# DFT over b and its inverse as eight array tiles of 64x32 and 32x64, with the spectral columns by parity of k

## The chip, the cores and the metric

The kernel runs on one core of a Trainium2 chip. The metric is the device time of one execution in microseconds (us). Engines are named as in the profile: PE is TensorE (PEld its weight loads), DVE is VectorE, ACT is ScalarE, POOL is GpSimd, SP is SyncE, which here only issues DMAs.

## The reference

Two branches work on the same x of 1 x 2048 x 512 in bf16, and a gate per row mixes them:

```python
g = sigmoid((x * gate_w).sum(-1, keepdims=True))
a = irfft2(rfft2(x, axes=(-2, -1)) * (w_r + 1j * w_i), s=(2048, 512)).astype(bfloat16)
h = einsum("bsd,df->bsf", x, w1) + b1            # d = 512, f = 1792
b = einsum("bsf,fd->bsd", h * tanh(softplus(h)), w2)
return g * a + (1 - g) * b
```

w_r and w_i are 2048 x 257, so branch a is a spectral filter over both axes; branch b is a dense layer with the Mish activation.

## The kernel before, in words

**Branch b** is dense. `mm1` (L810) multiplies w1 with the transposed x in four chunks of 512 rows, 14 row tiles each, four matmuls of 512 columns to a tile; ACT applies Mish (L819); `mm2` (L851, and L833 for the last row tile) multiplies back with 14 matmuls to each of 16 row tiles, in two parts of seven. Before the input is there, dummy matmuls (L509) keep PE going.

**Branch a** is the two-dimensional DFT as matmuls. The row index is s = 32a + b with 64 values of a and 32 of b.
- `tr` (L522) transposes x; DVE forms sums and differences (L537); `a1` (L551, L552, L554) is the real DFT over the 512 columns, 16 row tiles through PSUM bank 0, and eviction `e1` writes it to `In1` (in `Abuf`). The spectrum has 257 columns k; the real columns 0 and 256 are packed together, so that 256 are stored.
- `s1` (L572) is the DFT over a with its twiddle, in four batches, and gives 64 values e for every b. `e2` writes them to `Y1` (in `Ybuf`), and the DMAs `r1w` take them to DRAM (`scr1`) in four steps. `r1r` reads them back in another order into `In2` (in `Abuf`), so that b lies on the partitions.
- `s2` (L689) is the DFT over b in four batches n = 0 to 3, into PSUM banks 0 to 3. DVE multiplies by w_r and w_i (`wm`, L699, eight of 512 elements a batch), POOL or DVE adds or subtracts (`wz`, L705), and `s2i` (L732) is the inverse DFT over b, into the same banks. Eviction `e4` writes it to `T2s` (in `Ybuf`), the DMA `r2w` to DRAM (`scr2`), and eight DMAs `r2r` read it back as `T2r`.
- `s1i` (L764) and `a1i` (L776) are the inverses over a and over the columns; ACT scales by the gate (L781), DVE and POOL add the halves (L784), and branch b is added (L861, L869).

Columns k = 0 and 256 are real in the column direction and share a place; `s2x` (L664 to L666) separates them once, with small matmuls on the first column of `In2` and on its mirror image, which takes a reversed copy of the DFT matrix in `RR` (made by POOL in `rr`). DVE takes the result (`rs`, L711, and `x0`, L671 to L674), POOL multiplies it by the weights (`zq` to `z0i`), and `wc` (L722) writes it as column 0 of `Zb`, which `s2i` reads.

Before, the partitions of `In2` hold b (32) times real and imaginary part times two values of an index m2, and a matrix `RF` of 128 x 64 maps them to 32 outputs times the same two. Input and output with different m2 don't mix, so half of the matrix is zeros. `s2` uses it as two column halves of the array, `RI` of the inverse as two row halves:

```python
e.matmul(ps[64 * h:64 * h + 64, SB[i], 256 * c:256 * c + 256], RF[:, c, :], In2[:, 16 * h + u0 + i, :], ...)
```

with i over 4, c over 2 (real and imaginary output) and h over 2: sixteen matmuls of 256 columns a batch, in `s2` and in `s2i`.

**The order of the work** on each engine is fixed when the kernel is built. Each step is a task with an estimated time and with the buffers that it reads and writes; a list scheduler (`_Graph.schedule`) plays the engines and DMA queues through, takes among the steps that can start soonest the one of highest priority (the spectral steps stand above `mm1` and `mm2`), and so writes down each engine's order, which the engine then follows with semaphore waits. `evict` and `wz` may go to either of two engines, whichever is done first by the estimate. SP issues most of the DMAs in the order so planned: the input, `r1w`, `r1r`, two small ones of the gate (`gdj`), the constants of the inverse (`ld_g1`), `r2w`, `r2r` and the output. POOL issues the loads of the spectral weights (`ld_W`, into `WT`) and of w2.

Of the kernel before, what the change touches and what calls it, by code (L numbers as in the profile page):

```python
# [7 lines left out]
BF = mybir.dt.bfloat16  # L8
# [9 lines left out]
KR = 256  # L18

# [16 lines left out]
def _build_consts():  # L36
    cs = {}
# [21 lines left out]
    for kc in range(2):  # L59
        for half in range(2):  # L60
            kk = 4 * np.arange(64, dtype=np.float64)[:, None] + kc + 2 * half
            an = 2 * np.pi * kk * n / D
            GD[64 * half:64 * half + 64, 2 * kc, :] = 2 * np.cos(an)
            GD[64 * half:64 * half + 64, 2 * kc + 1, :] = -2 * np.sin(an)
# [5 lines left out]
    e = np.arange(64, dtype=np.float64)[None, :]  # L70
    M1 = np.zeros((128, 16, 2, 128))
    G1 = np.zeros((128, 32, 128))
    for b in range(32):
        bx, t = divmod(b, 16)
        ph = -2 * np.pi * e * (32 * a + b) / S
        c_, s_ = np.cos(ph), np.sin(ph)
        rows = slice(64 * bx, 64 * bx + 64)
        M1[rows, t, 0, 0:64] = c_
        M1[rows, t, 0, 64:128] = s_
        M1[rows, t, 1, 0:64] = -s_  # L80
        M1[rows, t, 1, 64:128] = c_
        ci, si = np.cos(-ph).T, np.sin(-ph).T
        G1[0:64, b, 0:64] = ci
        G1[64:128, b, 0:64] = -si
        G1[0:64, b, 64:128] = si
        G1[64:128, b, 64:128] = ci
    cs["M1"] = M1
    cs["G1"] = G1
    RF = np.zeros((128, 2, 64))
    RI = np.zeros((128, 2, 128))  # L90
    for b in range(32):
        for dd in range(32):
            ph = 2 * np.pi * b * dd / 32
            c_, s_ = np.cos(ph), np.sin(ph)
            for m2 in range(2):
                re_in, im_in = 4 * b + m2, 4 * b + 2 + m2
                o = 2 * dd + m2
                RF[re_in, 0, o] = c_
                RF[im_in, 0, o] = s_
                RF[re_in, 1, o] = -s_  # L100
                RF[im_in, 1, o] = c_
                for h in range(2):
                    i = 64 * h + o
                    RI[i, 0, re_in] = c_
                    RI[i, 0, im_in] = s_
                    RI[i, 1, re_in] = -s_
                    RI[i, 1, im_in] = c_
    P1 = np.zeros((128, 128))
    P0 = np.zeros((128, 128))

    def px(h, dd, m2):
        return 64 * h + 2 * dd + m2

    for h in range(2):
        for dd in range(32):
            for m2 in range(2):
                o = px(h, dd, m2)
                P1[px(1 - h, 31 - dd, 1 - m2), o] = 1
                u = 2 * m2 + h
                if u == 0:  # L120
                    P0[px(0, (32 - dd) % 32, 0), o] = 1
                else:
                    P0[px((4 - u) % 2, 31 - dd, (4 - u) // 2), o] = 1
    cs["SM"] = np.concatenate([RF.reshape(128, 128), RI.reshape(128, 256), P1, P0], axis=1)
# [198 lines left out]
def _build(nc, A_x, A_w_r, A_w_i, B_x, B_w1, B_b1, B_w2, gate_w, out):  # L323
# [6 lines left out]
    scr1 = nc.dram_tensor("scr1", (32, 128, KR), BF)  # L330
# [4 lines left out]
    with es:  # L335
# [13 lines left out]
        sm = sb("sm", [128, 640], BF)  # L349
# [18 lines left out]
        RR = sb("RR", [128, 2, 2, 64], BF)  # L368
# [12 lines left out]
        Zb = miscb[:, 4096:8192].rearrange("p (b u c n) -> p b u c n", b=2, u=4, c=2)  # L381
# [5 lines left out]
        RF = sm[:, 0:128].rearrange("p (c m) -> p c m", c=2)  # L387
        RI = sm[:, 128:384].rearrange("p (c m) -> p c m", c=2)
        P1m = sm[:, 384:512]
        P0m = sm[:, 512:640]  # L390
        In1 = Abuf[:, 0:8192].rearrange("p (t k) -> p t k", t=NT)
        In2 = Abuf[:].rearrange("p (j k) -> p j k", j=32)
        T2r = Abuf[:, 0:8192].rearrange("p (b k) -> p b k", b=32)
        Y1 = Ybuf[:].rearrange("p (b k) -> p b k", b=32)
        T2s = Ybuf[:, 0:8192].rearrange("p (h g k) -> p h g k", h=2, g=16)
# [8 lines left out]
        Wv = [w.rearrange("(m h g) k -> h m (g k)", h=2, g=16) for w in (A_w_r, A_w_i)]  # L404
        scr1_w = scr1.rearrange("b q k -> q b k")
        scr1_r = scr1.rearrange("b (m j) k -> (b m) j k", m=4)
        scr2_w = scr2.rearrange("b (m h g) k -> (b m) h (g k)", m=4, h=2)
# [85 lines left out]
        dma("ld_sm", sm[:], d_SM[:], writes=["sm"], nbytes=128 * 1280)  # L493
        dma("ld_gw", gwb[:, :], gate_w.unsqueeze(0).to_broadcast([128, 512]), writes=["gw"], nbytes=128 * 1024)
        dma("ld_gd", GDs[:], d_GD[:], writes=["GD"], nbytes=128 * 2048)
        for i in range(2):
            for h in range(2):
                dma(f"ld_W{i}{h}", WT[64 * h:64 * h + 64, i, :, :].rearrange("p g k -> p (g k)"), Wv[i][h],
                           writes=[("W", i, h)], nbytes=64 * 8224, queue="pool", deps=[t_w1])
        WALL = [("W", i, h) for i in range(2) for h in range(2)]  # L500
# [47 lines left out]
        for t in range(NT):  # L548
            def f_a1(e, t=t):
                pr = ps[:, 0, :].rearrange("p (r x) -> p r x", r=4)  # L550
                e.matmul(pr[:, 0, :], Tb[:, 0, t, :], FDs[:, 0:128], start=True, stop=True)  # L551
                e.matmul(pr[:, 2, :], Tb[:, 1, t, :], FDs[:, 128:256], start=True, stop=True)  # L552
                for i in range(2):
                    ins = e.matmul(pr[:, 1::2, :], Tb[:, 2 + i, t, :], FDs[:, 256 + 256 * i:512 + 256 * i].rearrange("p (r x) -> p r x", r=2),  # L554
# [5 lines left out]
            evict(f"e1_{t}", 512, In1[:, t, :].rearrange("p (c r q) -> p c r q", c=2, r=4),  # L560
                  ps[:, 0, :].rearrange("p (r c q) -> p c r q", r=4, c=2),
# [21 lines left out]
            if t % 4 == 3:  # L583
                for bx in range(2):
                    b0 = 16 * bx + t - 3
                    t_r1w.append(dma(f"r1w{t}_{bx}", scr1_w[:, b0:b0 + 4, :], Y1[:, b0:b0 + 4, :],
                                     reads=[("Y1", b0 + i) for i in range(4)], writes=[("scr1", b0 + i) for i in range(4)],
                                     nbytes=128 * 4 * 512, prio=SP0 + 1.0))
# [28 lines left out]
        def f_rr(e):  # L617
            v = RF.rearrange("p c (d m) -> p c d m", m=2)
            o = RR[:, 1].rearrange("p c (d m) -> p c d m", m=2)
            e.tensor_copy(out=RR[:, 0], in_=RF[:, :, ::-1])  # L620
            e.tensor_copy(out=o[:, :, :, 1], in_=v[:, :, ::-1, 1])
            e.tensor_copy(out=o[:, :, 0:1, 0], in_=v[:, :, 0:1, 0])
            return e.tensor_copy(out=o[:, :, 1:32, 0], in_=v[:, :, 31:0:-1, 0])

        G.add("rr", "pool", 1.2, f_rr, reads=["sm"], writes=["rr"])
# [16 lines left out]
        for hf in range(2):  # L642
            for h in range(2):
                j0 = 16 * h + 8 * hf
                t_r1r.append(dma(f"r1r{hf}{h}", In2[:, j0:j0 + 8, :], scr1_r[:, j0:j0 + 8, :],
                                 reads=[("scr1", b) for b in range(32)], writes=[("In2", j0 + i) for i in range(8)],
# [7 lines left out]
        SB = (0, 1, 2, 3)  # L654
        BSB = [("bank", i) for i in SB]
        xps = ps[:, 0, 0:64].rearrange("p (v c g) -> p v c g", v=2, c=2)

        def f_s2x(e):
            ins = None
            for c in range(2):  # L660
                for h in range(2):
                    o = xps[64 * h:64 * h + 64, :, c, :]
                    hr = 16 * (1 - h)
                    e.matmul(o[:, 0, :], RF[:, c, :], In2[:, 16 * h:16 * h + 16, 0], start=True, stop=True)  # L664
                    e.matmul(o[:, 1, 1:16], RR[:, 0, c, :], In2[:, hr + 15:hr:-1, 0], start=True, stop=True)
# [315 lines left out]
```

## Time and profile before

| what | value |
|---|---|
| three runs, median | 142.38 us (142.16 to 142.72) |
| the profiled execution | 142.56 us |
| its span, from the first to the last instruction | 140.8 us |
| PE busy | 136.2 us |
| DVE busy | 86.3 us |
| ACT busy | 81.4 us |
| POOL busy | 31.9 us |
| s2 (L689): 64 matmuls of 256 columns | 4.3 us busy |
| s2i (L732): 64 matmuls of 256 columns | 4.2 us busy |
| moved by DMA | 21.38 MB |

The profile is of one execution. A group of the profile is a line, an engine, an operation and its tiles; `128*64 128x256` is a matmul with a weight tile of 128 rows and 64 columns and a moving operand of 128 partitions by 256 columns. Matmuls overlap, and their ends are modelled, so their rate is read from the chain, from the starts, and not from the time of one. The chain that ended last is followed back from the last instruction, at each step to what released it; its times add up to the span.

### The profile page before, as it was taken

How to read it: one execution, taken by the hardware profiler on the slowest of the kernel's cores; microseconds unless marked ns; L12 is line 12 of the kernel's file. 1: busy time of each engine (PE TensorE's matmuls, PEld its weight loads, DVE VectorE, ACT ScalarE, POOL GpSimd, SP SyncE). 2: the span in 40 equal slices, each digit the busy share in tenths (PEclk: the TensorE clock that was granted, in tenths of full speed). 3: DMA queues.
4: the chain of work that ended last, by engine and by line, in shares of the span. 5: the costliest groups of instructions: out<-in, count | busy, mean ns of one | idle time of the engine just before them, and what ended most of it. 6: DMA issues, size and time to landing. Idle time of an engine off the chain costs nothing.

```text
span 140.8 us, 2515 instructions
## 1 busy us (share of the span) xinstructions
PE 136.2 (97%) x946; PEld 74.2 (53%) x946; DVE 86.3 (61%) x192; ACT 81.4 (58%) x128; POOL 31.9 (23%) x62
## 2 busy tenths in 40 slices
PE   6999999999999999999999999999999999999991
PEld 4756656455544435435445444544444666766670
DVE  0276757748999303983983893592200499999831
ACT  4448797969874487488058437532411685776300
POOL 4000670003000001560440440340000144256400
PEclk9999999999999999999999999999999999999999
DMA  3999999999705485700300300300359615333422
GB/s 87 334 382 387 393 245 214 239 333 366 222 8 154 151 254 202 289 0 10 143 0 0 149 0 5 149 2 0 143 150 277 179 27 119 80 79 92 98 52 58
DMA packets 16556, 21.38 MB, mean 152 GB/s; under 512 B 1248, under 2 KB 12384, under 8 KB 16160
## 3 DMA queue, kind: packets, MB, share of 16 engines
q1 hardware_dynamic: 15552, 17.22, 39.3%
q0 software_dynamic: 832, 3.94, 10.4%
q8 instruction: 7, 0.11, 0.3%
q10 hardware_dynamic: 160, 0.07, 0.2%
q14 instruction: 5, 0.04, 0.1%
HBM read 14.92 MB, written 6.29 MB: 151 GB/s over the span
## 4 chain that ended last, share of the span: by engine, by line
PE 92%; ACT 4%; DVE 0%; issue 0%
PE ps L810 33%; PE ps L851 32%; PE ps L776 5%; PE ps L509 3%; PE ps L689 3%; PE ps L572 3%; PE ps L732 3%; PE ps L764 3%; PE ps L522 2%; ACT Ybuf L452 2%; PE ps L833 2%; PE ps L554 2%; ACT act L819 1%; PE ps L551 1%; ACT Abuf L452 1%; ACT xT L452 1%
## 5 line engine op out<-in xcount | busy, mean ns | idle before, releaser
L810 PE MATMUL ps<-xT,w_sb 128*128 128x512 bf16 x224 | 54.2, 380 | 0.4 <-ACT act L819 0.3
L819 ACT ACTIVATE act<-ps,b1f 128x512 bf16<-128x512 f32 x56 | 38.1, 690 | 21.8 <-PE ps L810 16.4
L851 PE MATMUL ps<-w_sb,act 128*128 128x512 bf16 x210 | 48.3, 379 | 0.0
L810 PEld LDWEIGHTS ps<-xT,w_sb 128*128 128x128 bf16 x224 | 20.0, 98 | 24.1 <-ACT act L819 5.7
L851 PEld LDWEIGHTS ps<-w_sb,act 128*128 128x128 bf16 x210 | 20.1, 98 | 22.4 <-issue 0.4
L699 DVE TENSOR_TENSOR misc<-ps,WT 128x512 f32<-128x512 f32 x32 | 19.9, 685 | 12.6 <-PE ps L689 12.6
L705 POOL TENSOR_TENSOR misc<-misc 128x255 bf16<-128x255 f32 x16 | 11.4, 731 | 41.0 <-DVE misc L699 41.0
L784 POOL TENSOR_TENSOR Tg<-misc 128x256 bf16<-128x256 f32 x12 | 10.3, 873 | 27.9 <-ACT misc L781 27.9
L790 ACT ACTIVATE xo<-ps,omg 128x512 bf16<-128x512 f32 x11 | 7.6, 687 | 15.2 <-PE ps L851 15.0
L451 DVE CAST Ybuf<-ps 128x512 bf16<-128x512 f32 (+1 forms) x10 | 8.8, 900 | 9.3 <-PE ps L732 8.2
L781 ACT ACTIVATE misc<-ps,gcol 128x512 f32<-128x512 f32 x16 | 10.3, 685 | 5.0 <-PE ps L776 4.0
L451 DVE CAST misc<-ps 128x512 bf16<-128x512 f32 x8 | 5.5, 683 | 11.4 <-PE ps L764 11.4
L784 DVE TENSOR_TENSOR Tg<-misc 128x256 bf16<-128x256 f32 x20 | 12.0, 629 | 0.7 <-ACT misc L781 0.7
L594 DVE SCALAR_TENSOR_TENSOR junk<-xo,gwb 128x512 bf16<-128x512 bf16 x16 | 11.0, 689 | 0.7
L452 ACT ACTIVATE Ybuf<-ps 128x512 bf16<-128x512 f32 (+1 forms) x14 | 9.4, 718 | 2.6 <-PE ps L572 1.6
L451 DVE COPY xT<-ps 128x512 bf16<-128x512 bf16 x10 | 4.2, 424 | 9.1 <-PE ps L522 9.0
L776 PE MATMUL ps<-GDs,misc 128*128 128x256 bf16 x64 | 9.3, 273 | 0.0
L452 ACT ACTIVATE Abuf<-ps 128x512 bf16<-128x512 f32 x12 | 7.2, 602 | 0.0
L776 PEld LDWEIGHTS ps<-GDs,misc 128*128 128x128 bf16 x64 | 6.0, 98 | 2.3
L522 PEld LDWEIGHTS ps<-pid,xo 128*128 128x128 bf16 x64 | 5.2, 110 | 3.0 <-issue 0.4
L522 PE MATMUL ps<-pid,xo 128*128 128x128 bf16 x64 | 6.7, 242 | 0.0
L705 DVE TENSOR_TENSOR misc<-misc 128x255 bf16<-128x255 f32 x16 | 6.4, 441 | 0.0
(81 smaller groups left out, 115.7 us busy)
## 6 DMA issues: line engine op xcount, KB each, us to landing
scr<-Ybuf SPq DMA_DIRECT2D x8, 256.0 KB, 9.3
Abuf<-scr SPq DMA_DIRECT2D x4, 512.0 KB, 4.5
scr<-Ybuf SPq DMA_DIRECT2D x4, 512.0 KB, 3.0
Abuf<-scr SPq DMA_DIRECT2D x8, 256.0 KB, 5.3
w_sb<-in_B_w_dram POOLq DMA_DIRECT2D x2, 896.0 KB, 17.5
out_dram<-xo SPq DMA_DIRECT2D x14, 128.0 KB, 2.3
w_sb<-in_B_w_dram SPq DMA_DIRECT2D x3, 512.0 KB, 7.9
xo<-in_A_x_dram SPq DMA_DIRECT2D x3, 512.0 KB, 8.7
```

The lines of the kernel that those rows point to most:

```text
L451: G.add_multi(name, [("dve", dve_dur(n), lambda e: e.tensor_copy(out=dst, in_=src)), ("act", act_dur(n), lambda e: e.activation(dst, src, ...
L452: ("act", act_dur(n), lambda e: e.activation(dst, src, AF.Copy))],
L522: ins = e.transpose(psb[:, tbk, 128 * dt_:128 * (dt_ + 1)], xo[:, t, 128 * dt_:128 * (dt_ + 1)], perm[:, :])
L594: lambda e, t=t: e.scalar_tensor_tensor(out=junk[:, :], in0=xo[:, t, :], scalar=1.0, in1=gwb[:, :], op0=ALU.mult, op1=ALU.mult, accum_out= ...
L699: lambda e, Pb=Pb, Wu=Wu, bk=bk, pb=pb: e.tensor_tensor(out=Pb[:, pb, :].rearrange("p (c r q) -> p c r q", c=2, r=4), in0=ps[:, bk, :].rea ...
L705: fz = (lambda e, c=c, Pb=Pb, op=op, pb=pb, i=i, zb=zb: e.tensor_tensor(out=Zb[:, zb, i, c, 1:256], in0=Pb[:, pb, 1:256], in1=Pb[:, pb, 25 ...
L776: ins = e.matmul(ps[:, yk, 256 * (j // 2):256 * (j // 2) + 256], TT[:, ts_, j, :], GDs[:, j, :], start=(j % 2 == 0), stop=(j % 2 == 1))
L781: lambda e, t=t, gb=gb, yk=yk: e.activation(gEO[:, gb, :], ps[:, yk, :], AF.Copy, scale=gcol[:, t:t + 1]),
L784: fg = (lambda e, i=i, op=op, t=t, gb=gb: e.tensor_tensor(out=ga[:, t, 256 * i:256 * i + 256], in0=gEO[:, gb, 0:256], in1=gEO[:, gb, 256:5 ...
L810: ins = e.matmul(ps[:, bank, :], w1_sb[:, dt_, 128 * ft:128 * (ft + 1)], xT[:, dt_, 4 * c:4 * c + 4, :], start=(dt_ == 0), stop=(dt_ == 3))
L819: lambda e, ft=ft, bank=bank, hb=hb: e.activation(act[:, hb, ft, :], ps[:, bank, :], AF.Mish, bias=b1f[:, ft:ft + 1]),
L851: ins = e.matmul(ps[:, bank, :], act[:, hb, ft, 128 * tl:128 * (tl + 1)], w2_sb[:, ft, :], start=(ft == 0), stop=(ft == NFT - 1))
```

## The change

Three things are changed together.

- **The spectral columns** are ordered by the parity of k (`kk = 128 * half + 2 * i + kc`) where they were ordered by k mod 4. `a1` writes its outputs to PSUM in another arrangement, `e1` writes `In1` at a step of two elements, and `wm` reads the weights at a step of two in place of four.
- **The values e** are split in another way, into a half h (2), a quarter q (4) and a place u (8). The partitions of `In2` are now (h, b, real or imaginary), and its free axes q and u.
- **The DFT over b** is then a dense matrix of 64 x 32 (b and part in, 32 real or imaginary values out), and its inverse one of 32 x 64. `s2` runs on two row halves and four column quarters of the array, `s2i` on four row quarters and two column halves, with 512 columns to a matmul. The number of matmuls in a batch stays at sixteen.

With that go: `s2x` with 40 small matmuls in place of 12, waiting for the readers of two banks in place of one; `rs` as three copies in place of one; `rr` as three copies in place of four; 16 `r1w` DMAs of half the size in place of 8; `r2w` as eight in place of four; `ld_W` as eight in place of four; other pieces in `r1r` and `r2w`; and other estimates for the scheduler.

```diff
-            kk = 4 * np.arange(64, dtype=np.float64)[:, None] + kc + 2 * half
+            kk = 128 * half + 2 * np.arange(64, dtype=np.float64)[:, None] + kc
...
-    RF = np.zeros((128, 2, 64))
-    RI = np.zeros((128, 2, 128))
+    RF = np.zeros((128, 2, 32))
+    RI = np.zeros((128, 2, 64))
...
-        Wv = [w.rearrange("(m h g) k -> h m (g k)", h=2, g=16) for w in (A_w_r, A_w_i)]
-        scr1_w = scr1.rearrange("b q k -> q b k")
-        scr1_r = scr1.rearrange("b (m j) k -> (b m) j k", m=4)
-        scr2_w = scr2.rearrange("b (m h g) k -> (b m) h (g k)", m=4, h=2)
+        Wv = [w.rearrange("(m q g) k -> q m (g k)", q=4, g=16) for w in (A_w_r, A_w_i)]
+        scr1_w = scr1.rearrange("h b m k -> h m b k")
+        scr1_r = scr1.rearrange("h b (c q u) k -> (h b c) q (u k)", c=2, q=4)
+        scr2_w = scr2.rearrange("b (c h q u) k -> h (b c) q (u k)", c=2, h=2, q=4)
...
-            for h in range(2):
-                dma(f"ld_W{i}{h}", WT[64 * h:64 * h + 64, i, :, :]...
+            for q in (0, 2, 1, 3):
+                dma(f"ld_W{i}{q}", WT[32 * q:32 * q + 32, i, :, :]...
...
-            evict(f"e1_{t}", 512, In1[:, t, :].rearrange("p (c r q) -> p c r q", c=2, r=4),
-                  ps[:, 0, :].rearrange("p (r c q) -> p c r q", r=4, c=2),
+            evict(f"e1_{t}", 512, In1[:, t, :].rearrange("p (x q i) -> p x i q", x=4, i=2),
+                  ps[:, 0, :].rearrange("p (i x q) -> p x i q", i=2, x=4),
...
-                    t_r1w.append(dma(f"r1w{t}_{bx}", scr1_w[:, b0:b0 + 4, :], Y1[:, b0:b0 + 4, :], ...
+                    for h in range(2):
+                        t_r1w.append(dma(f"r1w{t}_{bx}{h}", scr1_w[h][:, b0:b0 + 4, :], Y1[64 * h:64 * h + 64, b0:b0 + 4, :], ...
...
             for c in range(2):
-                for h in range(2):
-                    o = xps[64 * h:64 * h + 64, :, c, :]
-                    hr = 16 * (1 - h)
-                    e.matmul(o[:, 0, :], RF[:, c, :], In2[:, 16 * h:16 * h + 16, 0], start=True, stop=True)
-                    e.matmul(o[:, 1, 1:16], RR[:, 0, c, :], In2[:, hr + 15:hr:-1, 0], start=True, stop=True)
-                    ins = e.matmul(o[:, 1, 0:1], RR[:, 1 - h, c, :], In2[:, 16 * h:16 * h + 1, 0], start=True, stop=True)
+                for q in range(4):
+                    for h in range(2):
+                        o = xps[32 * q:32 * q + 32, h, :, c, :]
+                        r = slice(64 * h, 64 * h + 64)
+                        e.matmul(o[:, 0, :], RF[r, c, :], In2[r, q, :, 0], start=True, stop=True)
+                        ins = e.matmul(o[:, 1, :], RR[r, 0, c, :], In2[r, 3 - q, :, 0], start=True, stop=True)
+                    ins = e.matmul(xps[32 * q:32 * q + 32, 0, 1, c, 0:1], RR[0:64, int(q == 0), c, :], In2[0:64, (4 - q) % 4, 0:1, 0], ...
...
-                for i in range(4):
-                    for c in range(2):
+                for c in range(2):
+                    for q in range(4):
                         for h in range(2):
-                            ins = e.matmul(ps[64 * h:64 * h + 64, SB[i], 256 * c:256 * c + 256], RF[:, c, :], In2[:, 16 * h + u0 + i, :],
+                            r = slice(64 * h, 64 * h + 64)
+                            ins = e.matmul(ps[32 * q:32 * q + 32, 2 * h + c, :], RF[r, c, :], In2[r, q, 2 * n:2 * n + 2, :].rearrange("p u k -> p (u k)"),
                                            start=True, stop=True)
...
-                for i in range(4):
-                    for c in range(2):
+                for c in range(2):
+                    for q in range(4):
                         for h in range(2):
-                            r = slice(64 * h, 64 * h + 64)
-                            ins = e.matmul(ps[:, 2 * (i // 2) + h, 256 * (i % 2):256 * (i % 2) + 256].rearrange("p (j i q) -> p j i q", j=2, i=2), RI[r, c, :],
-                                           Zb[r, zb, i, c, :].rearrange("p (i j q) -> p j i q", j=2, i=2), start=(c == 0), stop=(c == 1))
+                            r = slice(32 * q, 32 * q + 32)
+                            ins = e.matmul(ps[64 * h:64 * h + 64, q, :], RI[r, c, :], Zb[r, zb, h, c, :, :].rearrange("p u n -> p (u n)"),
+                                           start=(c == 0), stop=(c == 1))
...
-            t_r2w.append(dma(f"r2w{n}", scr2_w[:, :, 1024 * n:1024 * (n + 1)], ...
+            for h in range(2):
+                t_r2w.append(dma(f"r2w{n}{h}", scr2_w[h][:, :, 512 * n:512 * n + 512], ...
```

## The prediction

> **What bounds the kernel now.** I read the page's busy shares first, then the chain that ended last, then the groups of instructions with shapes kept apart, and last the timeline around one batch of the steps that change. The page:
>
> ```profile
> span 140.8 us, 2515 instructions
> PE 136.2 (97%) x946; PEld 74.2 (53%) x946; DVE 86.3 (61%) x192; ACT 81.4 (58%) x128; POOL 31.9 (23%) x62
> PEclk9999999999999999999999999999999999999999
> PE 92%; ACT 4%; DVE 0%; issue 0%
> ```
>
> TensorE is occupied from start to end at its full granted clock, and the chain is 92% TensorE. Work taken off it shortens the run, as long as enough other matmuls stand ready to fill the waits of the spectral path. The stages by the table of stretches say that this filling works: between 53.9 and 98.3 us, where the changed steps lie, PE is busy 44.40 of 44.40 us, DVE 30.24, ACT 23.25, POOL 13.76.
>
> The chain, in order of time, around the first s2, s2x and s2i:
>
> ```profile
> 53.12 0.86 PE ps L810 x4
> 53.98 0.99 PE ps L689 x16
> 54.97 1.62 PE ps L851 x7
> ...
> 57.45 0.14 PE ps L664 x2
> ...
> 63.21 0.98 PE ps L732 x16
> 64.19 1.83 PE ps L810 x8
> ...
> 110.92 0.44 PE ps L776 x4
> ```
>
> Four 512-column matmuls take 0.86, so 0.216 each; four 256-column ones (L776) take 0.44, so 0.109 each. Sixteen of 256 columns would need 1.74 one after another; s2 (L689) and s2i (L732) need 0.98. So two tiles already work at once: 8 x 0.109 = 0.87, and 0.11 is left over. The work behind is late by the same amount: L851 x7 takes 1.62 against 1.51 elsewhere in the chain, L810 x8 1.83 against 1.73. So a batch costs 0.87 of streaming and about 0.2 for going into and out of the tiled mode. The timeline, cut at 53.95, 54.05 and 54.156 us, shows the pairs:
>
> ```profile
> 53.91 0.30 PE L689 MATMUL ps<-Abuf,sm 128*64 128x256 bf16 x2
> 53.91 0.41 PE L689 MATMUL ps<-Abuf,sm 128*64 128x256 bf16 x4
> 53.91 0.52 PE L689 MATMUL ps<-Abuf,sm 128*64 128x256 bf16 x6
> ```
>
> Two start together, the next two 0.11 later. In s2 the pair are two column halves with different moving data, in s2i two row halves; both run at the full rate.
>
> **The change, part by part.** *s2 and s2i, eight batches.* Before and after a batch has sixteen matmuls. After, they have 512 columns, and eight tiles can work at once (two row halves by four column quarters in s2, four row quarters by two column halves in s2i): two rounds of 0.216 = 0.43. To that comes the stagger of the starts within a round: the two of a pair start within 0.003 us in the trace, so seven steps are 0.02; in s2x, where small matmuls follow closely, two start each 0.03, which would be 0.11 for seven. I take 0.46, near the first, since the instructions are queued ahead of a batch. The mode switches stay at 0.2, as many as before. Gain: 0.87 - 0.46 = 0.41 a batch, 3.3 us for eight; between 2.6 (0.54 a batch) and 3.5. No row has more than two tiles at work, so the other end is no gain and even a loss; that is the first rival.
>
> Weight loads: after, each of the eight tiles of a round loads its own. The timeline cut at 53.915 and 53.945:
>
> ```profile
> 53.91 0.11 PEld L689 LDWEIGHTS ps<-Abuf,sm 128*64 128x64 bf16 x2 [0.42 <-issue]
> 53.91 0.14 PEld L689 LDWEIGHTS ps<-Abuf,sm 128*64 128x64 bf16 x4 [0.42 <-issue]
> ```
>
> Loads for two different tiles start together, the second load of the same tile 0.03 later. So I let the eight go side by side and charge nothing; if they had to queue at 0.03 each, the first round would wait 0.2 and the gain would be 0.2 a batch, 1.7 in all. The Trainium skill, "TensorEngine Tiling (Array Packing)", Restrictions and Gotchas, speaks against the change here: column tiling excludes the fast weight load. s2i had 128-column weights without column tiling (L732's loads take 94 ns, L689's 109) and now gets column tiling. By that rule with loads in a queue the sum would be the 1.7 just named; the pair starting together decides against it.
>
> *s2x* (column k=0, once) grows from 12 small matmuls to 40. Before: pairs start at 57.38, .44, .47, .50, .53 and .57, 0.03 apart on one tile, 0.2 us in all. After: eight groups of five, in each group two waits for a load on the same tile: 8 x 0.06 = 0.5; with half as many weight columns to load perhaps half of it; all forty in a row would be 1.2. I take 0.45, so +0.25, between +0.05 and +1.0. The same page's section on instruction overhead (about 60 cycles whatever the size) would give about 1.0 us, an estimate from its figure; the pairs 0.03 apart say 0.015 a matmul.
>
> *DVE, ACT.* wm (L699) has the same 32 instructions of 512 elements; W is read at a step of two elements in place of four. The step of four costs nothing now: 685 ns against 683 for a plain cast of the size (L451). e1 writes at a step of two elements where it wrote runs of 64; no row shows a strided write on ACT or DVE. By the read it costs nothing, which I take; at worst it doubles 12 x 602 and 4 x 692 ns. e4 and wz keep their sizes. rs goes from one copy of 187 ns to three, +0.25 on DVE (starts of the neighbouring small ones are 0.09 apart), once. s2x now waits for four wm (two banks, 2.5 us) where it waited for two, but s2 itself ends 0.41 sooner; so the first s2i, which waits for z0 through POOL, comes 0 to 0.8 us later against a path 0.41 shorter. PE has mm1 to run meanwhile (24 matmuls, 5.5 us, lie there now), so this costs nothing; without that cover, up to 0.8.
>
> *DMA issues.* On SP r1w goes from 8 to 16 and r2w from 4 to 8, with the same bytes. Behind the last r1w stand r1r, gdj and ld_g1 on SP, and s2 waits for r1r. The last r1w pair is issued at 42.3 and 42.9 in 0.36 each; two more cost about 0.7. The second r1r waits behind gdj anyway, is issued at 48.5, lands at 52.7, and s2 starts at 53.9: 1.2 of slack hides it. Behind the last r2w stand the eight r2r; it lands 3.0 after its issue at 99.6; one more issue (0.5) and pieces of 1 KB in place of 2 KB may make it a microsecond later. The first two r2r land at 105.6 and 106.4, s1i starts at 108.8, and 10.7 us of mm2 fill the hole. Cover gone, each would cost its delay. On POOL the W loads go from four to eight of 0.52 to 0.60: up to +2.2 before the w2 loads, which land at 36.8 and are first used at 43.3; W lands at 31.8 and serves POOL's small column sums and, from 55 us on, DVE. Nothing charged; rr loses a copy.
>
> *Sum.* -3.3 + 0.25 = -3.05. The profiled execution took 142.56 (140.8 span and 1.8 around it), 0.18 over the median 142.38. So span 137.7, time 139.5 by the profiled run and 139.3 by the median. The order of the engines is planned anew with the new durations; a single wait of PE for ACT in the present order costs about 0.3, so I add 0.5 to either side. The likeliest case's own range is 138.4 to 141.2.
>
> **Rivals.**
> 1. *Slower: the eight tiles don't stream together.* The place is TensorE's operand supply: s2 now asks every row half for four different moving streams, s2i writes four banks from four row quarters. With four of eight at once a batch takes 4 x 0.216 = 0.86 and nothing is gained; that is where it turns. With two, 1.73, so +0.86 a batch and +6.9 in all: 149.5. For it: no row shows more than two. Against: pairs on either axis run without any loss. With exactly four: 142.6, no change.
> 2. *Half a gain.* Only one of the two shapes reaches eight: -1.65 + 0.25, so 141.0. Or all weight loads queue: -1.7 + 0.25, so 140.9.
> 3. *Stage one pays.* e1's strided write is slow. Bank 0 carries a1, then e1, one after the other, a1 to a1 1.41 apart in the chain (9.17, 10.58, 12.00); 0.3 more each over 16 is +4.8, so 144.1. Only the untested write speaks for it.
> 4. *The gain is hidden.* If the chain s2, wm, wz, s2i, e4 on DVE set the end, s2's share would still shorten it, so it would give 1.5 to 3; it falls in the ranges above. PE's 97% speaks against even that.
>
> **How the numbers follow.** Likeliest, eight at once: 0.68. Rival 2: 0.10. Four at once, or gain and loss even: 0.08. Rival 1 with two: 0.07; rival 3, or a wait in the new order that costs more than the gain: 0.07. A measurement of this kernel tells 0.5% (0.7 us) from no change. Faster: 0.78; the same: 0.08; slower: 0.14. The range reaches from the likeliest's low end, 138.4, over rival 2 up to 142.0; what lies above are the slower cases and part of the even one.
>
> **What would show it.** Right: the batches of L689's and L732's successors take about 0.58 in the chain in place of 0.98, eight matmuls start within 0.05 us, PE stays at 97% of a span near 137.7, s2x takes about half a microsecond, and the Abuf evictions stay at 602 ns on ACT. Wrong: starts in groups of two or four; PE below 95% with waits for DMA ahead of s2 or s1i; Abuf evictions above 700 ns on ACT.

## The result, and the profile after

| | before | after |
|---|---|---|
| median, measured side by side | 142.50 us (142.16 to 142.72, four runs) | 141.11 us (140.46 to 143.34, four runs) |
| the profiled execution, its span | 142.56, 140.8 us | 141.29, 139.6 us |

The ratio is 0.9889 [0.9845, 0.9934]: the kernel is faster by 1.1%, which is 1.6 us; the two medians differ by 1.4. A few executions are disturbed and run longer than the others (of after's four the one of 143.34), and ratios and means, here and below, are formed without them. The forecast was 139.3, within a range from 138.4 to 142.0; of the 3.1 us that it expected, about half came. The profiled execution is the longest of the three that count for after: their spans are 139.6, 139.2 and 138.7, so a difference of a few tenths between two single spans says little.

The page of after, its busy shares and the shares of the chain:

```profile
span 139.6 us, 2608 instructions
PE 133.5 (96%) x974; PEld 69.3 (50%) x974; DVE 86.4 (62%) x194; ACT 82.2 (59%) x128; POOL 33.2 (24%) x65
PE 87%; ACT 5%; DMA 4%; SPq 1%; issue 0%; DVE 0%
```

PE is busy for 2.7 us less, yet the span is only 1.2 shorter. The chain has two entries that it didn't have before, DMA with 4% and SP's queue with 1%. The chain of before, from the first to the last s1 (start, length, what):

```profile
14.83 1.00 PE ps L572 x16
...
17.43 0.49 ACT Abuf L452
...
40.44 0.98 PE ps L572 x16
```

and the chain of after, in order of time:

```profile
14.88 1.00 PE ps L559 x16
...
17.48 0.64 ACT Abuf L439
...
40.91 0.98 PE ps L559 x16
...
48.75 0.52 SPq L408
...
49.31 0.60 SPq L408
...
49.95 5.65 DMA Abuf<-scr
55.60 0.14 issue
55.73 0.63 PE ps L685 x16
...
63.81 0.64 PE ps L730 x16
```

Three things are to be read here.

- The batches of s2 (now L685) and s2i (L730) take 0.63 and 0.64 where they took 0.99 and 0.98. The later six take 0.56 or 0.57. The eight sum to 4.66 us against 7.88: -3.2. The first two hold some waiting: from the start of a batch to the start of the work behind it, all eight take 0.56 or 0.57 (before 0.98 to 1.00), together 4.51 against 7.91: **-3.4**.
- Between the first and the last s1 (L559, before L572) lie 26.03 us, where before it was 25.61 (14.83 to 40.44): **+0.42**. In the same part of the chain the eviction by ACT to `Abuf`, which is e1, stands twice with 0.64 where it stood with 0.49.
- The first s2 hangs on a DMA: the second of the four `r1r`, issued at 49.95 behind two other issues of SP, lands 5.65 later, and PE stops for it. Before, PE was busy right up to the first s2, and this place of the chain was mm1 and mm2 from 41.4 to 53.98.

The stop in the table of waits of after (line, what it waited for, us in total, times, the longest); before has no such row:

```profile
PE ps L685 <- DMA Abuf<-scr: 1.3, 1, 1.3
```

By the starts it is a little more. The last matmul ahead of s2 starts 1.67 before the first of s2, 1.45 more than the pace of 0.22; but before it was 0.31, since going into the tiled mode takes 0.09, so PE loses **1.36** us. (The expectations below speak of 1.45; the stops given for other runs are over 0.31, as here.) s2x adds 0.12, with 0.42 in place of 0.30, and 0.2 is left for other waits, as of PE for ACT (two of together 0.5 us, where one of 0.3 was). -3.4 + 0.42 + 1.36 + 0.12 + 0.2 is -1.3, the difference of the spans (140.82 and 139.56).

The timeline of after, cut at 55.76, 0.03 after the first s2 has begun:

```profile
55.73 0.41 PE L685 MATMUL ps<-Abuf,sm 64*32 64x512 bf16 x8 [1.29 <-DMA Abuf<-scr]
```

Eight matmuls are under way at once. Their starts are 3.3 ns apart, and those of the second round come 0.215 after the first, which is the pace of one 512-column matmul. So the eight tiles cost each other nothing.

The groups with shapes kept apart show e1 (ACT, then DVE), first of before and then of after:

```profile
L452 ACT ACTIVATE Abuf<-ps 128x512 bf16<-128x512 f32 x12 | 7.2, 602 | 0.0
L451 DVE CAST Abuf<-ps 128x512 bf16<-128x512 f32 x4 | 2.8, 692 | 2.0 <-PE ps L554 2.0
...
L439 ACT ACTIVATE Abuf<-ps 128x512 bf16<-128x512 f32 x12 | 9.0, 752 | 0.0
L438 DVE CAST Abuf<-ps 128x512 bf16<-128x512 f32 x4 | 2.9, 732 | 2.0 <-PE ps L541 2.0
```

The step of two elements in the write costs ACT a quarter more and DVE 6%.

The last `r1w` issues on SP, and how long they take to land, of before:

```profile
L421 SPq DMA_DIRECT2D scr<-Ybuf x2: 359/359/359, 42.3 to 42.9; - x2
DMA to landing us min/median/max: 2.3/2.5/2.6
```

and of after:

```profile
L408 SPq DMA_DIRECT2D scr<-Ybuf x4: 574/596/629, 42.7 to 44.7; - x4
DMA to landing us min/median/max: 2.4/2.5/3.5
```

A half of 64 partitions takes SP 0.6 us to issue, a whole of 128 partitions 0.36. There are four in a row in place of two, and the last one also lands later, after 3.5 us. So the last `r1w` lands at 48.24, before at 45.47.

Why the last one takes a microsecond longer stands in the trace's DMA packets. A DMA is cut into packets that 16 DMA engines move; these `r1w` packets hold 512 bytes, and an engine's share of one `r1w` is 16 of them. The trace also has packets of a kind that it calls instruction, of 16 KB, on a queue of their own (q8), seven in the whole run. One of them runs from 46.12 to 47.09, and three stretches of after's DMA packets around it, 46.1 to 46.15, 46.85 to 47.06 and 47.06 to 47.85, hold:

```profile
q8 instruction: 1, 0.02, 120.1%
...
DMA packets 0, 0.00 MB, mean 0 GB/s; under 512 B 0, under 2 KB 0, under 8 KB 0
...
DMA packets 17, 0.01 MB, mean 10 GB/s; under 512 B 1, under 2 KB 17, under 8 KB 17
```

No packet of `r1w` starts between 46.85 and 47.06, and then one engine's share, 16 packets and the small one that reports the landing, goes through alone. 15 of the 16 engines had reported by 47.19, and the last one reports at 48.24. The trace doesn't name a packet's engine, but the share starts as the 16 KB end, so the reading is that this packet held one engine, and the rest of the last `r1w` waited behind it. The other runs agree: each one in which the two meet has such a last engine, and no other has. Before, the like packet runs from 45.19 to 46.23, and from 45.13 to 46.3 it is the only one:

```profile
DMA packets 1, 0.02 MB, mean 14 GB/s; under 512 B 0, under 2 KB 0, under 8 KB 0
q8 instruction: 1, 0.02, 5.5%
```

There the last `r1w` packet had started at 45.12, and so was just clear of it.

### The profile page after: what moved, and what is told of

Its sections match the earlier page's. It is cut to its first block, busy times and chain, and to the rows that moved or that the text cites. A ratio compares the mean times of both kernels' runs of the same rounds, so it can differ in the third digit from the quotient of the medians.

```text
span 139.6 us, 2608 instructions
## 1 busy us (share of the span) xinstructions
PE 133.5 (96%) x974; PEld 69.3 (50%) x974; DVE 86.4 (62%) x194; ACT 82.2 (59%) x128; POOL 33.2 (24%) x65
## 4 chain that ended last, share of the span: by engine, by line
PE 87%; ACT 5%; DMA 4%; SPq 1%; issue 0%; DVE 0%
PE ps L849 32%; PE ps L808 30%; PE ps L774 5%; DMA Abuf<-scr 4%; PE ps L496 3%; PE ps L559 3%; PE ps L762 3%; PE ps L509 2%; ACT Ybuf L439 2%; PE ps L831 2%; PE ps L541 2%; PE ps L730 2%; PE ps L685 2%; SPq L408 1%; ACT Abuf L439 1%; PE ps L538 1%
## 5 line engine op out<-in xcount | busy, mean ns | idle before, releaser
L439 ACT ACTIVATE Abuf<-ps 128x512 bf16<-128x512 f32 x12 | 9.0, 752 | 0.0
L541 PE MATMUL ps<-FDs,Tg 128*128 128x256 bf16 x32 | 6.1, 272 | 0.0
```

The lines of the kernel that those rows point to most:

```text
L439: ("act", act_dur(n), lambda e: e.activation(dst, src, AF.Copy))],
```

## The experiments

The theory after the result: the tiles give what was forecast, and two costs take half of it back, the halves of `r1w` on SP's queue (a stop of PE ahead of s2) and e1's strided write (stage one, from the first to the last s1). The rival: the tiles give less than the chain shows, and the stop only stands where other waits stood before, so that it would cost nothing to have it.

### Splitting r1w alone, on the kernel before (before_r1w_split)

```diff
-  t_r1w.append(dma(f"r1w{t}_{bx}", scr1_w[:, b0:b0 + 4, :], Y1[:, b0:b0 + 4, :], ...
+  for h in range(2):
+      t_r1w.append(dma(f"r1w{t}_{bx}{h}", scr1_w[64 * h:64 * h + 64, b0:b0 + 4, :], Y1[64 * h:64 * h + 64, b0:b0 + 4, :], ...
```

> The kernel before with nothing changed but r1w as 16 DMAs of 64 partitions; tiles, r1r and everything else as before. Theory A: each r1w issue takes about 0.6 us on SP in place of 0.36, the first r1r is issued after 47.0 in place of 45.6, PE stops for 0.7 to 1.5 us ahead of the first s2, span 141.5 to 142.3, slower by 0.5 to 1%. Theory B: no stop above 0.3 us, span 140.5 to 141.1, no change in time.

Measured: 144.07 us (143.76 to 144.64, six runs) against 142.52, ratio 1.011 [1.0087, 1.0134]; span 142.5. The chain ahead of the first s2 (here L690):

```profile
49.60 5.92 DMA Abuf<-scr
...
55.66 1.06 PE ps L690 x16
```

The stop is there with nothing else of the change, 1.63 us by the starts, and the whole time grows by 1.6. The instruction packet is in the way here too (45.77 to 46.75): 15 engines have reported the last `r1w` by 46.80, the last one reports at 47.94. Against this kernel, which shares the split with after, after's span is 2.9 shorter, and 3.2 in the mean of the executions (139.2 against 142.4), e1's 0.4 already paid: the tiles are worth 3.3 to 3.6, where the starts say 3.4. That ends the rival.

### The same number of DMAs over all partitions (before_r1w_by_b)

Also on the kernel before: sixteen `r1w`, each of 128 partitions and two values of b, in place of 64 partitions and four.

```diff
+  b1 = b0 + 2 * h
+  t_r1w.append(dma(f"r1w{t}_{bx}{h}", scr1_w[:, b1:b1 + 2, :], Y1[:, b1:b1 + 2, :], ...
```

> The kernel before with r1w as 16 DMAs of 128 partitions and two values of b each: as many issues and bytes as with halves of 64 partitions, on all partitions; the rest as before. Theory A, the shape is what costs (64 partitions: 0.57 to 0.63 us an issue, a last landing 3.6 us after its issue): 0.36 an issue, last r1w landed by 46.4, first r1r issued by 46.5, no stop above 0.4 us ahead of the first s2, span 140.6 to 141.2. Theory B, the number of issues costs: last landing after 47.2, a stop of 0.8 us or more, span above 141.6, as with the halves (142.5).

Measured: 143.51 us (142.15 to 144.47, twelve runs) against 142.49, ratio 1.004 [1.0011, 1.0069]. The times lie in two groups, five from 142.15 to 142.63 and seven from 143.48 to 144.47, and the profile is of one of the upper group. In it the issues take 0.36 to 0.49, and the first three of the last four `r1w` have landed by 45.60; the fourth, issued at 44.12, lands at 47.88. Its first DMA engine is done at 45.87, its last one two microseconds later. The other 15 are done by 46.07, 0.6 later than the whole `r1w` of the kernel before. So the shorter issues alone don't settle it: what makes `r1r` late in this profile is one lagging engine of the last transfer, and again the instruction packet (45.90 to 46.85) is in its way: no other packet starts between 45.72 and 46.83, and three of 512 bytes come after it. That the lower group of times are the executions in which the last `r1w` gets through ahead of this packet would fit, but it isn't shown, since one execution alone was traced; the experiment stays undecided between the number of issues and their shape.

### The last lower halves on another queue (r1w_two_queues)

On the kernel after; ACT issues the lower halves of the last four `r1w`.

```diff
-  nbytes=64 * 4 * 512, prio=SP0 + 1.0))
+  nbytes=64 * 4 * 512, prio=SP0 + 1.0, queue="act" if t == 15 and h == 1 else "sp"))
```

> The changed kernel with the two lower-half r1w DMAs of the last s1 batch issued by ACT in place of SP; all else, r1r too, as it is, and PE's order the same. Theory A, four issues of 0.6 us in a row on SP set the start of r1r: the last r1w lands near 46.3 in place of 48.2, the second r1r is issued near 49.0 and lands before 54.2, PE's stop ahead of the first s2 falls from 1.45 to below 0.4 us, span 138.2 to 138.6, ratio to before 0.980. Theory B, halves of 64 partitions move slowly whoever issues them: the last lands after 47.3, the stop stays above 0.9, span above 139.0.

Measured: 139.70 us (139.59 to 140.46, five runs) against 142.18, ratio 0.9837 [0.9813, 0.9862]; span 137.9. The chain ahead of the first s2:

```profile
53.20 0.86 PE ps L808 x4
54.07 0.60 PE ps L685 x16
```

mm1 runs into s2 again, as before the change. The last `r1w` lands at 46.57, the second `r1r` is issued at 48.54 and lands at 52.97. ACT pays 0.66 and 0.73 us for its two issues, and PE's waits for ACT stay at 0.5 as in after. The span is 1.7 shorter than after's in the profiled executions, and 1.0 in the mean of all that count (138.1 against 139.2); the ratios differ by 0.5%, 0.7 us. So the stop was a cost, and didn't merely stand in the place of other waits, but the 1.36 of the one execution is more than its mean. This kernel gets rid of two things at once: the row of four issues, and the instruction packet (45.85 to 46.89), which holds up nothing of `r1w`, whose last packets start by 45.99.

### gdj behind r1r (gdj_behind)

On the kernel after; the two small DMAs `gdj` stand behind the four `r1r` on SP.

```diff
-        for bx in range(2):
-            dma(f"gdj{bx}", ...
...
+        # after the four r1r:
+        for bx in range(2):
+            dma(f"gdj{bx}", ...
```

> The changed kernel with the two gdj DMAs behind the four r1r on SP in place of between the first and the second; r1w in 16 pieces as it is. The second r1r is issued at 48.8 in place of 49.95 and lands near 54.4. The planner puts 24 mm1 ahead of s2 in place of 20 mm1 and 7 mm2, 0.65 us less, so part of a stop stays: theory A, 0.7 to 1.1 us of it, since r1w's end still sets the start of r1r, span 138.6 to 139.2. Theory B, gdj alone made the stop: it goes below 0.3 us and the span to 138.2.

Measured: 140.09 us (139.38 to 141.01, six runs) against 142.18, ratio 0.9853 [0.9822, 0.9884]; span 138.6. The chain:

```profile
48.54 5.50 DMA Abuf<-scr
...
54.18 0.63 PE ps L688 x16
```

The second `r1r` goes 1.4 earlier, at 48.54, and the stop falls to 0.7, though PE has 0.65 less to do ahead of s2 in this order (24 mm1 in place of 20 mm1 and 7 mm2). The span is 1.0 shorter, in the profiled executions and in the mean. So the place behind `gdj` was a part of the stop, and the late `r1w` (it lands at 48.03 here, behind an instruction packet that ends at 46.85) the other. How the two share it isn't shown.

### r1w whole, r1r in partition halves (r1w_whole)

On the kernel after; `scr1` is stored so that `r1w` goes out in eight DMAs of 128 partitions as before, and `r1r` pays for it, reading 64 partitions at a time.

```diff
-        M1[rows, t, 0, ma + 32] = s_
+        M1[rows, t, 0, mb + 64] = s_
...
-                t_r1r.append(dma(f"r1r{hf}{qp}", In2[:, 2 * qp:2 * qp + 2, 4 * hf:4 * hf + 4, :]...
+                t_r1r.append(dma(f"r1r{hf}{hh}", In2[64 * hh:64 * hh + 64, :, 4 * hf:4 * hf + 4, :]...
```

> The changed kernel with r1w as 8 DMAs of 128 partitions again (rows of scr1 reordered, r1r read in two partition halves with the same 2 KB pieces). Theory A, the end of r1w is late because it is issued in 16 pieces: the first r1r is issued near 46.0 in place of 48.3, PE's stop of 1.45 us ahead of the first s2 falls below 0.3, span near 138.2, time about 1.4 us under the changed kernel's, ratio to before 0.98. Theory B, the r1r themselves are slow with 2 KB pieces in place of 4 KB: the stop stays above 1.0 and the span above 139.2.

Measured: 140.59 us (140.09 to 141.26, six runs) against 142.52, ratio 0.9865 [0.9837, 0.9894]; span 138.5. The chain:

```profile
54.17 0.56 PE ps L684 x16
...
58.07 0.59 issue
58.66 0.23 PE ps L650 x6
```

The stop ahead of s2 is gone (the first `r1r` is issued at 45.78), and a new one of about 0.6 stands ahead of s2x (L650), which needs all four `r1r`. These land at 51.06, 53.88, 56.29 and 58.57. Reads of 512 KB into 64 partitions land 2.3 to 2.8 apart; before, into 128 partitions, the last three landed 1.3 apart, and in after, with the same 2 KB pieces as here, 1.3 to 1.4. So the number of partitions is what slows them, and not the pieces. A part of the cost went from one half of the round trip to the other: the mean span is 138.7, 0.5 below after's.

### e1 contiguous, the step moved to a1's write in PSUM (e1_plain)

On the kernel after; the DFT over the columns writes PSUM at a step of two, and e1 copies straight.

```diff
-  pr = ps[:, 0, :].rearrange("p (i c j q) -> p j i c q", i=2, c=2, j=2)
+  pr = ps[:, 0, :].rearrange("p (c j q i) -> p j i c q", i=2, c=2, j=2)
...
-  evict(f"e1_{t}", 512, In1[:, t, :].rearrange("p (x q i) -> p x i q", x=4, i=2),
-        ps[:, 0, :].rearrange("p (i x q) -> p x i q", i=2, x=4),
+  evict(f"e1_{t}", 512, In1[:, t, :], ps[:, 0, :],
```

> The changed kernel with a1 writing PSUM at a step of two, so that e1 reads and writes without a step. Theory A, e1's write at a step of two elements made stage one longer: Abuf evictions on ACT go from 752 back to about 600 ns, the last s1 batch comes 0.45 us earlier (40.84 to 40.4), and the span falls by as much, to about 139.1, since the wait ahead of s2 is moved along. Theory B, a1's step in PSUM costs PE what e1 gains: a1's two wide matmuls take more than 0.22 us in the chain and the last s1 batch stays at 40.8.

Measured: 145.35 us (144.55 to 146.21, six runs) against 142.52, ratio 1.0209 [1.0171, 1.0246]; span 143.4. e1 is back at 602 ns on ACT, and the kernel is slower by far. The chain shows where:

```profile
9.04 0.11 PE ps L539
9.15 0.43 PE ps L541 x2
```

Two 256-column matmuls of a1 take 0.43, in after 0.22, and one of 128 columns 0.11 in place of 0.06. A step of two in the fp32 that a matmul writes doubles its time. Sixteen row tiles by 0.32 are 5 us, and the span is 4.2 above what after's would be without its 0.4 for e1. Runs of 64 values, as in after, cost nothing. The Trainium skill, "PSUM — Partial Sum Buffer", Specifications (TRN2), says that PSUM has 8-byte lines and that a pattern which isn't contiguous slows matmuls considerably; this run gives the factor, two at a step of two, and the runs of 64 show that not every break in the pattern counts.

### Both of these (both)

> Both edits in the changed kernel. If the two losses are separate: span about 137.7, that is 139.6 less 1.45 less 0.45, time 139.3, ratio to before 0.978. If they are one loss seen twice: no better than the better of the two alone.

Measured: 144.75 us (144.06 to 145.87, six runs), ratio 1.0166 [1.0125, 1.0206]; span 143.3. a1's doubled time decides here too, and it hides what the `r1w` part gives alone.

### The strided e1 alone, on the kernel before (before_e1_step)

The same step in e1's write, on the kernel before; this changes the order of the spectral columns in `In1`, and the steps behind it are left as they are.

```diff
-  evict(f"e1_{t}", 512, In1[:, t, :].rearrange("p (c r q) -> p c r q", c=2, r=4),
+  evict(f"e1_{t}", 512, In1[:, t, :].rearrange("p (x q i) -> p x i q", x=4, i=2),
```

> The kernel before with e1 writing at a step of two elements, nothing else changed; the spectral columns are then in another order than the weights expect. Theory A, the write at a step costs 150 ns on ACT and 40 on DVE, and stage one passes it on: Abuf evictions 750 ns, the first matmul of the last s1 batch at 40.8 in place of 40.4, span 141.2 to 141.4. Theory B, mm1 hides it: Abuf evictions 750 ns and a span of 140.8.

Measured: 142.62 us (142.46 to 143.09, ten runs) against 142.18, ratio 1.0028 [1.0009, 1.0046]. The chain from the first to the last s1:

```profile
14.55 1.00 PE ps L572 x16
...
40.60 0.98 PE ps L572 x16
```

That is 26.05 against 25.61, with e1 at 752 on ACT and 734 on DVE: 0.44 in the trace, 0.4 in the times. The span is only 0.1 longer than before's, since the first mm1 of this execution began 0.28 earlier (6.98 against 7.26).

### Columns by k mod 4 again (columns_mod4)

On the kernel after, with the tiles kept: the columns are ordered as in the kernel before, e1 writes runs of 64, and s2i reads its operand in another order, 256 columns to a matmul, 32 matmuls a batch.

```diff
-            kk = 128 * half + 2 * np.arange(64, dtype=np.float64)[:, None] + kc
+            kk = 4 * np.arange(64, dtype=np.float64)[:, None] + kc + 2 * half
...
+                for uu in range(2):
...
+                                ins = e.matmul(ps[64 * h:64 * h + 64, q, 256 * uu:256 * uu + 256].rearrange("p (j i q) -> p j i q", j=2, i=2), RI[r, c, :], ...
```

> The changed kernel with the spectral columns by k mod 4 as before, so that e1 writes runs of 64; s2i then reads Zb and writes PSUM in runs of 64 and takes 32 matmuls of 256 columns a batch in place of 16 of 512, on the same eight tiles. Abuf evictions back to 600 ns, last s1 batch 0.45 us earlier; theory A, eight tiles hold their rate with 256 columns, 0.57 to 0.62 us a batch of s2i in the chain, span 139.1 with the stop ahead of s2 still there. Theory B, 32 instructions a batch are limited by their issue: more than 0.75 a batch, span 139.6 or more.

Measured: 140.79 us (140.34 to 141.63, four runs) against 142.18, ratio 0.9904 [0.9874, 0.9935]; span 139.9. e1 is at 602 and 692 again and stage one at 25.61 (14.92 to 40.53). But the chain goes on with

```profile
49.55 6.36 DMA Abuf<-scr
...
56.05 0.62 PE ps L685 x16
```

The stop has grown to 2.05, and what stage one won is gone. The second `r1r` was issued 0.4 earlier, and took 6.36 in place of 5.65. This is the longest of the four executions, but their mean span, 139.15, is after's 139.17 too. So here the work saved ahead of the transfers brought nothing; why they took longer was not found. The s2i batches of 32 matmuls of 256 columns take 0.57 in the chain, but for the first with 0.64, so they keep the rate.

### Both repairs together (queues_and_mod4, queues_mod4_gdj)

The edits of r1w_two_queues and columns_mod4 in one kernel; the second one also has that of gdj_behind.

> Both mendings in the changed kernel: the last r1w halves on two queues, and the spectral columns by k mod 4. If the stop and stage one are separate losses: no stop ahead of s2, stage one (first to last s1 batch) 25.6 us in place of 26.05, and 0.45 us less than with the two queues alone: time 139.2, ratio to before 0.980. If s2's stop only comes back because stage one ends sooner: same time as with two queues, 139.7.

> The same with the gdj DMAs behind the r1r too. With no stop left, an earlier r1r has nothing more to give: within 0.2 us of the kernel with both mendings, 139.2. If there is still a wait on r1r that the chain does not show: 0.4 us less, 138.8.

Measured: 139.40 us (139.03 to 139.47, five runs) against 142.54, ratio **0.9778 [0.9755, 0.9801]**, span 137.7; with `gdj` behind, 139.62 (139.38 to 139.71, four runs), ratio 0.9797 [0.9775, 0.9819], span 138.0. The chain of the first:

```profile
14.79 1.00 PE ps L559 x16
...
40.40 0.98 PE ps L559 x16
...
53.07 0.86 PE ps L809 x4
53.94 0.61 PE ps L685 x16
```

25.61 for stage one, no stop ahead of s2, and the batches at their new length. This is the best kernel of the study, clear of after's interval, and 3.1 us ahead of the kernel before: the whole sum of the prediction, and its span of 137.7. That it agrees to a tenth is in part luck, since the batches gave 0.1 more than forecast, s2x cost 0.13 less, and other waits took 0.2. With the second queue there is nothing left for `gdj` to win.

### A tile's two matmuls in a row (tile_by_tile)

On r1w_two_queues; in s2 and s2i the two matmuls of one tile follow each other in the program, where a round over all tiles came first.

```diff
-                for c in range(2):
-                    for q in range(4):
-                        for h in range(2):
+                for q in range(4):
+                    for h in range(2):
+                        for c in range(2):
```

> The changed kernel with r1w on two queues, and the sixteen matmuls of a batch of s2 and s2i in another order: the two matmuls of a tile one after the other, then the next tile, so that at most two tiles work at once. Theory A, starts are in order and the gain comes from eight tiles working at once: nine steps of 0.216 a batch, 1.95 in the chain in place of 0.57, and PE is late by about 1.4 a batch, 11 us in all: span about 149. Theory B, the array takes the other tiles' matmuls ahead of a waiting one: batches stay at 0.57 to 0.7 and the span at 138.

Measured: one execution of 141.25 us with a span of 138.0, beside 137.9 for r1w_two_queues; a single time says nothing of 0.5%, so the span and the batches are what is read. The timeline, cut at 54.0:

```profile
53.92 0.43 PE L685 MATMUL ps<-Abuf,sm 64*32 64x512 bf16 x8
```

Eight at once again, with starts 6.7 ns apart in place of 3.3, and a batch of 0.58 to 0.67. If matmuls had to start in the order of the program, the second of a tile would hold up the other tiles, and a batch would go tile after tile. They don't: a matmul that waits for its own tile lets those of other tiles pass. The same is in after's s2x, where the chain has five of one line (L651) ahead of the L652 that stand between them in the program. The Trainium skill, "TensorE: Matmul & The Clock Gate", Part 3: Packing small matmuls, has matmuls start strictly in program order; these starts differ, and the measurement decides.

## Why the prediction was right or wrong, by its own steps

**The batches: right.** The gain of 0.41 for each of eight was the largest term and the riskiest. Measured: 3.4 in all for the forecast 3.3, starts 3.3 ns apart, a batch of 0.56 to 0.64 in the chain for the forecast 0.58. Weight loads for eight tiles start 3.3 ns apart as well; the 1.7 that queued loads would have left is not seen, nor a loss from the weight loading rule that was weighed against the trace. Rivals 1 and 2 fall with this.

**s2x: a cost of half the size taken.** +0.12 in place of +0.25, with 40 matmuls in 0.42. The 0.45 taken for after was near; the 0.2 for before was too low, since the chain has 0.29 there.

**"Two more cost about 0.7 ... 1.2 of slack hides it": this step failed**, and it is the stop of 1.36. The slack was read rightly, but the last `r1w` lands 2.77 late and not 0.7. Stage one and the start account for 0.48 of this (the first issue of the row is at 42.75 in place of 42.27). The issues account for 1.35: their price was that of the 128-partition form, 0.36, and the halves take 0.6, so from the first to the last issue of the four it is 1.95 where two took 0.60. The last 0.94 is the last transfer, 3.54 from issue to landing in place of 2.60, which the instruction packet explains: 15 engines were done 2.49 after the issue. The profile of before didn't show this, since there the last `r1w` was clear of that packet by 0.07. And "waits behind gdj anyway" overlooked that the first `r1r` stands ahead of `gdj` on the queue: it waits for the last `r1w`, and holds up `gdj` and all that follows. Before, `gdj`'s own data were late (47.24) and hid this. From the two traces, for the second `r1r`:

| us | before | after |
|---|---|---|
| last `r1w` issued | 42.87 | 44.70 |
| it lands | 45.47 | 48.24 |
| first `r1r` issued | 45.55 | 48.33 |
| second `r1r` issued | 48.48 | 49.95 |
| it lands | 52.67 | 55.60 |
| s2 starts | 53.98 | 55.73 |

It lands 2.9 late. 1.2 of that is the slack, 0.4 is stage one's, by which the path is late as well, and the 1.3 left is the stop. Splitting `r1w` alone brings the stop to the kernel before, and moving two issues takes it out of the kernel after. How much of the stop is the longer issues' and how much the instruction packet's no run shows, since every edit that removed the stop moved both; with 1.05 us between the 15th engine's report and the 16th's, the packet's part can be most of it. The second `r1r` takes 5.4 to 6.4 us from its issue in the kernels with the stop, where it took 4.2 (and 4.4 in r1w_two_queues). A part of that is its place: in after it is issued 1.62 behind the first `r1r` in place of 2.93, and lands 3.47 behind it, hardly longer than the 3.30 of before. Why this distance lies between 1.8 and 4.3 in the other kernels stays open.

**"By the read it costs nothing, which I take": this step failed too**, with 0.42 to 0.44. A read at a step on DVE was the nearest row, and it is no measure of a write on ACT: 602 to 752 is a quarter more. Rival 3 had the right place and the wrong size. It let the whole surplus fall on the path sixteen times; 12 x 0.15 and 4 x 0.04 are 2.0 us on the engines, and a fifth of that came through: 0.30 in two evictions by ACT that stand in the chain, less 0.10 by which the copies to `xT` behind them stand shorter there, and the rest in waits around a1. The bound had been named, but it was priced at nothing in the sum.

**Hidden as forecast:** `r2w` in eight, since the 49 matmuls of mm2 still stand for 10.68 us ahead of s1i and no wait is there; the W loads on POOL; `wm` at a step of two (680 ns for 685); `rs` as three copies of 151 to 158 ns.

The signs by which this could be seen were in the prediction's last part: a DMA wait ahead of s2, and evictions above 700 ns on ACT. Both came true, beside the right batches; PE went to 96%, and not below the 95% that was named with the wait.

## What to carry to other kernels

When a change splits a DMA, follow the last landing through everything that stands behind it on the issuing queue, in the order in which the queue has it, and ask which waiting issue would then be at its head; a slack read between two of its transfers isn't a slack of the queue. Look in the DMA packets for traffic of another kind near a landing that much depends on: a transfer that is clear of it by 0.07 us in one kernel runs into it in the next. Price an issue by a row with the same number of partitions, and a strided write by a strided write; where there is none, give it a term in the sum and a place in the range, and not nothing. Read more than one execution where a stop depends on such timing: single spans of after lie 0.9 apart. Where an order has to be changed on the way through PSUM, the eviction is the cheap place for the step and the matmul's write the dear one.

## What the runs showed of the hardware

- Eight tiles of 64x32 or 32x64 stream at once at the full pace, 16 matmuls of 512 columns in 0.43 and 0.02 of stagger; going into the tiled mode and out of it takes 0.09 each (0.31 in place of 0.22 from the last start ahead of a batch to its first, and from its last start to the first behind it). In tile_by_tile matmuls of other tiles pass one that waits for its own tile.
- A step of two in the fp32 that a matmul writes to PSUM doubles it: 0.216 against 0.109 for 256 columns.
- A bf16 write at a step of two costs ACT 752 ns for 602 (512 elements), DVE 732 for 692.
- On SP a DMA over 64 partitions takes 0.57 to 0.63 us to issue, over 128 partitions 0.36 in the same place (0.36 to 0.49 in before_r1w_by_b); reads of 512 KB into 64 partitions land 2.3 to 2.8 apart, into 128 1.3.
- A packet of kind instruction, 16 KB, takes a DMA engine 0.96 us in after and 1.04 before. In after, before_r1w_split, before_r1w_by_b, gdj_behind, columns_mod4 and e1_plain it met the last `r1w`, one engine of which then reported 1.05 to 1.81 us behind the other 15; in the kernels in which `r1w` got through ahead of it, at most 0.33.
